# A list scheduler inside a two-layer attention kernel: charging changes of the array's tiling, new durations and new offsets

## The chip, the core and the metric

The kernel runs on one core of a Trainium2 chip. Engines: TensorE (PE) multiplies, VectorE (DVE), ScalarE (ACT) and GpSimd (POOL) do the element-wise work, SyncE (SP) issues transfers. The metric is the device time of one execution in microseconds; a run's figure is compared by its median over several runs.

## What is computed

The reference is causal attention of 8 batches, 8 heads, 576 positions, head size 64, with sparse masks, followed by a second attention per "expert" whose results are gated:

```python
scores = scale * q @ k.T                       # per batch and head
masks: heads 0-3: 0 <= i-j < 32; heads 4-7: i >= j and i % 32 == j % 32
x = softmax(masked scores) @ v                 # heads joined: x is (8, 576, 512)
logits = x @ w_gate; topk = the 2 largest of 4; w = softmax over those two
for e in range(4):
    q, k, v = x @ wq[e], x @ wk[e], x @ wv[e]  # 512 -> 64
    ye = causal_softmax(scale * q @ k.T) @ v @ wo[e]
    out += (w of e, or 0) * ye
```

All values are float32. The kernel splits activations and weights of the second layer into a high and a low part (fp32r) and multiplies high by high, low by high and high by low, so each projection step is three matmuls.

## The kernel before

Nothing in the kernel is a loop in the order of execution. Functions declare operations with `op(kind, eng, key, fn, r, w, mode, npk)` (L188): the kind's name, the engines that may do it with a duration in us for each, a key, the function that emits the instructions, the buffers read and written, the tiling of the array for PE, and for a transfer its size. `schedule()` (L219) then keeps a model clock for each engine, and step by step takes the operation that can start first; among those of one engine that are ready within 0.02 us of each other it takes the lowest key. The function of the operation is called at that moment, so each engine's queue holds its instructions in the order of the plan. On the chip semaphores keep the order of data.

The key is a due time (batch number times T = 52 plus a place within the batch) plus two offsets from the table `PRI` (L107 to L185): one for the kind, one for the kind in that batch (the key is put together in L192). `LAT` (L217) is added behind an operation's end before a reader may start. Copies out of PSUM that either ACT or DVE may do have two durations, from `act(n)` and `dve(n)` (L324, L327).

Buffers come from rings (L84): a fixed number of tiles; an operation can't start until each buffer it uses has a tile. `RB` (L308) is PSUM: eight banks of 128 x 512 floats. `PTR` (one buffer) holds transposed probabilities of the first attention, `XH` and `XL` (five each) the high and low part of that attention's result.

Operations on PE, with the lines of their matmuls and the tiling (rows x columns) that they use, for each batch:

- `stage1`, four pairs of heads, two local and two strided: `tp` transposes of q and k (L529, 64x128), `s` scores (L561, 64x64), `pt` transposes of the probabilities (L619 local, L622 strided, 64x128), `xa` probabilities times values (L656 local, 128x64; L673 strided, 64x64). Between `s` and `pt` stand mask, maximum, subtraction, exponential, sum and scaling on DVE, POOL and ACT.
- `project`: `pj`, eight of twelve matmuls (L779; L790 in the first batch, where each is cut into four parts of three), `values2`: `vp`, five of twelve (L726), all 128x128.
- `attend`, for two pairs of experts and two groups of query tiles: `s2` scores (L864, 64x128) and `s2_4` for the last tile (L844, 128x128), `t2` transposes (L918, 64x128), `acc` probabilities times values (L951, 128x64).
- `out_tile`: `yp` (L980, 128x128), its copy and its store (L989 to L992).

A transposing operation writes two PSUM banks, each emptied by a copy on ACT or DVE (L334). In a batch there are 8 `tp`, 6 `pt` and 10 `t2`. Loads (L421 weights, L475 and L482 q and k, L503 to L514 v), the small gate copy (L764) and the stores all are issued from SP's queue.

The choice among ready operations, before:

```python
for rt, o in ready:
    if rt <= first + 0.02:
        k = o.key + (MODE_PEN if e == "PE" and mode not in (None, o.mode) else 0.0)
...
if e == "PE":
    if mode not in (None, o.mode):
        d += 0.09
    elif t > free[e] + 0.05:
        d += 0.08
...
MODE_PEN = 5.0
```

Of the kernel before, what the change touches and what calls it, by code (L numbers as in the profile page):

```python
# [20 lines left out]
def attention_moe_kernel(  # L21
# [45 lines left out]
    class Buf:  # L67


        def __init__(self, ring, name, root=None):  # L70
            self.ring, self.name = ring, name
            self.root = root or self
            self.writers, self.readers, self.parts = [], [], {}
            self.t, self.nops, self.freed, self.taken = None, 0, 0.0, False

# [5 lines left out]
    class Ring:  # L81


        def __init__(self, tag, shape, dtype, bufs, pool=None, tiles=None):  # L84
            self.tag, self.bufs = tag, bufs
            if tiles is None:
                tiles = [pool.tile(shape, dtype, name=f"{tag}{i}") for i in range(bufs)]
            self.tiles, self.holder = tiles, [None] * bufs

# [18 lines left out]
        "acc": 114.0, "acc 0": -309.5, "acc 1": 334.0, "acc 2": 0.5, "acc 3": -4.0, "acc 4": 65.5,  # L108
# [13 lines left out]
        "hi_w 0": -35.5, "lo_w": 81.0, "lo_w 0": -112.0, "load_qk": 4.0, "load_qk 0": -138.0,  # L122
        "load_qk 1": -69.5, "load_qk 2": 23.0, "load_qk 3": -12.0, "load_qk 4": -31.5, "load_qk 5": 38.5,
        "load_qk 6": 39.5, "load_qk 7": 61.5, "load_v": 80.0, "load_v 0": -111.0, "load_v 1": -7.0,
        "load_v 2": -4.0, "load_v 3": 2.5, "load_v 4": 91.0, "load_v 5": 65.5, "load_v 6": 39.5,
        "load_v 7": 28.0, "load_w": -16.5, "load_w 0": 55.5, "mask": -175.5, "mask 0": 162.0, "mask 1": 75.0,
# [10 lines left out]
        "pj_lo 6": -203.5, "pj_lo 7": 167.5, "pj_out": -95.5, "pj_out 0": -139.5, "pj_out 1": 101.5,  # L137
# [186 lines left out]
    def act(n):  # L324
        return 0.15 + 0.00083 * n
# [732 lines left out]
```

## Time and profile before

| | us |
|---|---|
| median of 3 runs | 489.04 |
| lowest and highest run | 488.28, 492.18 |
| span of the profiled execution | 488.3 |
| PE busy in it | 470.8 |
| DVE, ACT, POOL busy | 338.3, 307.4, 215.3 |

The span runs from the first to the last instruction of the profiled execution. A busy PE is one on which a matmul is in flight by the profiler's model; matmuls overlap, so the rate is read from the distance between the starts of two of them. In rows of the timeline "x12" means that twelve equal instructions behind each other were merged; the first number is the start, the second how long the row lasts.

### The profile page before, as it was taken

The page shows a single profiled execution, that of the slowest core. Times are in us where ns is not written, and L with a number is a line of the kernel's source. Part 1 is how long each engine was busy: PE and PEld are TensorE (multiplying, and loading weights), DVE is VectorE, ACT ScalarE, POOL GpSimd, SP SyncE. Part 2 cuts the span into 40 slices and gives each one's busy share as a digit, 9 for nine tenths or more (in the row PEclk, how much of TensorE's full clock was granted, in tenths as well). Part 3 has the DMA queues.
Part 4 walks back from the last instruction along what each step waited for, and adds up shares of the span by engine and source line. Part 5 has one row for each costly group of instructions (what it writes and reads, how often), then busy time and mean ns, then how long its engine had stood idle before and what let it go on. Part 6 is the DMA issues. An engine that isn't in the chain of part 4 may idle for free.

```text
span 488.3 us, 17766 instructions
## 1 busy us (share of the span) xinstructions
PE 470.8 (96%) x7142; PEld 409.5 (84%) x7142; DVE 338.3 (69%) x1037; ACT 307.4 (63%) x876; POOL 215.3 (44%) x315
## 2 busy tenths in 40 slices
PE   7579899999999999999999999999999999999996
PEld 6569788889789988799987999898878998799774
DVE  5497867887778678766669557856787856635740
ACT  3487678655575487855687647737777445845742
POOL 5377643461455146641446504463086425212530
PEclk9798999999999999999999999999999999999999
DMA  7866961702166015630247403510223300100014
GB/s 145 172 170 152 203 118 54 170 1 75 46 155 135 1 48 157 164 85 2 75 119 208 130 2 83 153 49 27 76 94 84 83 1 28 65 1 1 23 66 129
DMA packets 88881, 43.36 MB, mean 89 GB/s; under 512 B 77024, under 2 KB 80480, under 8 KB 88800
## 3 DMA queue, kind: packets, MB, share of 16 engines
q1 hardware_dynamic: 88800, 42.24, 34.4%
q8 instruction: 56, 0.92, 0.8%
q14 instruction: 25, 0.20, 0.1%
HBM read 32.78 MB, written 9.44 MB: 86 GB/s over the span
## 4 chain that ended last, share of the span: by engine, by line
PE 88%; DMA 5%; SPq 4%; DVE 1%; issue 1%; ACT 0%; DVEq 0%; ACTq 0%
PE bank L779 19%; PE bank L726 12%; PE bank L980 11%; PE bank L951 10%; PE bank L864 7%; PE bank L918 7%; PE bank L561 5%; PE bank L529 4%; PE bank L656 3%; DMA nat<-in_k_dram 3%; PE bank L844 3%; PE bank L673 2%; PE bank L619 2%; SPq L421 1%; PE bank L790 1%; PE bank L622 1%
## 5 line engine op out<-in xcount | busy, mean ns | idle before, releaser
L899 POOL TENSOR_SCALAR p<-p,st,wt 128x128 f32<-128x128 f32 (+3 forms) x128 | 76.0, 608 | 88.1 <-DVE st L883 53.1
L876 ACT ACTIVATE p<-p,st 128x128 f32<-128x128 f32 (+3 forms) x128 | 71.8, 562 | 11.2 <-DVE st L871 11.1
L871 DVE CUSTOM_DVE_ANT_0 p<-bank,m_cau 128x128 f32<-128x128 f32 (+3 forms) x128 | 55.9, 485 | 13.7 <-PE bank L864 13.7
L799 ACT CAST qk<-bank 128x288 fp32r<-128x288 f32 x64 | 25.5, 400 | 47.4 <-PE bank L779 45.0
L951 PE MATMUL bank<-th,vs 128*64 128x192 f32 (+4 forms) x512 | 50.4, 339 | 0.0
L334 ACT COPY qkt<-bank 128x324 f32<-128x324 f32 (+2 forms) x110 | 40.3, 425 | 14.5 <-PE bank L529 14.0
L334 ACT COPY th<-bank 128x256 f32<-128x256 f32 (+2 forms) x102 | 40.7, 425 | 11.8 <-PE bank L918 8.3
L726 PE MATMUL bank<-wl_v,xh 128*128 128x260 f32 (+1 forms) x160 | 45.3, 283 | 1.2 <-DVE wl_v L430 1.2
L726 PE MATMUL bank<-wh_v,xh 128*128 128x260 f32 (+1 forms) x160 | 46.2, 288 | 0.0
L951 PEld LDWEIGHTS bank<-th,vs 128*64 128x64 f32 x512 | 33.9, 136 | 13.6 <-issue 6.6
L726 PE MATMUL bank<-wh_v,xl 128*128 128x260 f32 (+1 forms) x160 | 45.2, 283 | 0.0
L334 DVE COPY th<-bank 128x384 f32<-128x384 f32 (+2 forms) x58 | 28.4, 496 | 23.6 <-PE bank L918 23.1
L801 DVE TENSOR_TENSOR qkl<-bank,qk 128x288 fp32r<-128x288 f32 x64 | 28.4, 451 | 21.4 <-ACT qk L799 21.0
L918 PEld LDWEIGHTS bank<-ident,p 64*128 64x128 f32 x800 | 31.8, 138 | 11.4 <-issue 5.8
L918 PE MATMUL bank<-ident,p 64*128 64x64 f32 x800 | 41.2, 230 | 0.1
L596 POOL TENSOR_TENSOR p1l<-p1l,st 128x960 f32<-128x960 f32 (+1 forms) x18 | 29.0, 1616 | 24.5 <-DVE st L594 16.4
L587 POOL TENSOR_TENSOR p1l<-p1l,st 128x960 f32<-128x960 f32 (+1 forms) x18 | 29.0, 1614 | 23.6 <-DVE st L585 20.2
L529 PE MATMUL bank<-ident,nat 54*128 54x54 f32 (+1 forms) x636 | 30.9, 231 | 7.4 <-DMA nat<-in_k_dram 4.4
L561 PE MATMUL bank<-qkt 64*64 64x54 f32 (+1 forms) x1408 | 34.1, 242 | 2.0 <-issue 0.7
L529 PEld LDWEIGHTS bank<-ident,nat 54*128 54x128 f32 (+1 forms) x636 | 25.3, 143 | 11.8 <-issue 3.6
L779 PE MATMUL bank<-xh,wh_k 128*128 128x288 f32 x112 | 34.2, 306 | 0.0
L641 ACT CAST xh<-bank 128x320 fp32r<-128x320 f32 (+4 forms) x80 | 26.9, 376 | 11.4 <-PE bank L656 6.1
(147 smaller groups left out, 1341.3 us busy)
## 6 DMA issues: line engine op xcount, KB each, us to landing
out_dram<-ys SPq DMA_DIRECT2D x32, 256.0 KB
v<-in_v_dram SPq DMA_DIRECT2D x32, 192.0 KB
nat<-in_q_dram SPq DMA_DIRECT2D x28, 144.0 KB
nat<-in_k_dram SPq DMA_DIRECT2D x28, 144.0 KB
nat<-in_q_dram SPq DMA_DIRECT2D x32, 99.0 KB
nat<-in_k_dram SPq DMA_DIRECT2D x32, 99.0 KB
v<-in_v_dram SPq DMA_DIRECT2D x48, 54.0 KB
nat<-in_q_dram SPq DMA_DIRECT2D x16, 90.0 KB
```

The costliest lines, as they stand in the source:

```text
L334: (nc.scalar.copy if e == "ACT" else nc.vector.tensor_copy)(dst, src)
L529: nc.tensor.transpose(tp[x].t[:, w_ * (g - g0):w_ * (g - g0) + w_], blk, ident[r, r])
L561: nc.tensor.matmul(o, lhs, rhs, start=True, stop=True)
L726: nc.tensor.matmul(vp.t[:m, :NV], xx.t[:, t0:t0 + m], ww.t[:, kt, :], start=i == 0, stop=i == 11)
L779: nc.tensor.matmul(pj.t[:, :HS], ww.t[:, kt, ep * 128:(ep + 1) * 128], xx.t[:, c], start=i == 0, stop=i == 11)
L864: nc.tensor.matmul(sp[a].t[:, :nk], x.t[r, 0, q0:q0 + 128], y.t[r, 1, :nk], start=i == 0, stop=i == 2)
L871: lambda e, sp=sp, p=p, a=a, nk=nk, ci=ci: nc.vector.tensor_tensor_reduce(out=p.t[:, a, :nk], in0=sp[a].t[:, :nk], in1=m_cau[:, S - nk:], ...
L876: op("exp2", {"ACT": 0.485 + 0.00083 * nk}, k_ + 1, lambda e, p=p, a=a, ci=ci, nk=nk: nc.scalar.activation(p.t[:, a, :nk], p.t[:, a, :nk], ...
L899: lambda e, p=p, a=a, ci=ci, t=t, nk=nk: nc.gpsimd.tensor_scalar(p.t[:, a, :nk], p.t[:, a, :nk], st.t[:, 14 + ci + a:15 + ci + a], wt.t[:, ...
L918: nc.tensor.transpose(tp[hf].t[:, 64 * c:64 * c + 64], src, ident[r, r])
L951: nc.tensor.matmul(acc.t[o, c0:c0 + cn], vw, th[a].t[:, s0:s0 + cn], start=j == 0, stop=j == idx[-1], skip_group_check=True)
L980: nc.tensor.matmul(yp.t[:, :DM], xx.t[:, c0:c0 + 128], ww.t[:, ep, :], start=i == 0, stop=i == 5)
```

## The change

The set of operations, their instructions and their transfers are the same. What differs is the scheduler's model and its choice:

- Among PE's ready operations, one of another tiling counts as ready `SWITCH` later, and the window of choice on PE is `WAIT_PE`. `MODE_PEN` is 614.376 instead of 5. A change of tiling costs 0.095 us plus a lead that depends on the new tiling, instead of 0.09.
- Durations of nearly all operations and `LAT` have new values.
- Transfers are modelled in us on two lanes, of which the strided loads use one.
- `PTR`, `XH` and `XL` are handed out in the order in which their buffers were made.
- All offsets of `PRI` are new; the old ones lie between -838 and 405, the new ones reach beyond -3000 and 2800.

The diff, cut (of the offsets and of the durations only examples are shown):

```diff
+            if ring and ring.fifo:
+                ring.order.append(self)
...
+            self.fifo, self.order = False, []
...
+            if self.fifo:
+                self.order.remove(buf)
...
-        "acc": 114.0, "acc 0": -309.5, "acc 1": 334.0, "acc 2": 0.5, "acc 3": -4.0, "acc 4": 65.5,
+        "acc": 0.0, "acc 0": -1082.0, "acc 1": 1878.0, "acc 2": -874.0, "acc 3": 176.0, "acc 4": 1208.0,
...
-    LAT = {"PE": 0.22, "ACT": 0.1, "DVE": 0.1, "POOL": 0.12, "SP": 0.0}
+    LAT = {"PE": 0.2, "ACT": 0.14, "DVE": 0.12, "POOL": 0.11, "SP": 0.0}
...
-        dma_free = 0.0
+        dma = [0.0, 0.0]
...
                         if not u.taken:
+                            if u.ring.fifo and u.ring.order[0] is not u:
+                                rt = None
+                                break
                             need[u.ring] = need.get(u.ring, 0) + 1
...
-                    first = rt if first is None else min(first, rt)
-                    ready.append((rt, o))
+                    other = e == "PE" and mode not in (None, o.mode)
+                    ef = rt + (SWITCH if other else 0.0)
+                    first = ef if first is None else min(first, ef)
+                    ready.append((ef, rt, o, other))
...
-                for rt, o in ready:
-                    if rt <= first + 0.02:
-                        k = o.key + (MODE_PEN if e == "PE" and mode not in (None, o.mode) else 0.0)
+                for ef, rt, o, other in ready:
+                    if ef <= first + (WAIT_PE if e == "PE" else 0.02):
+                        k = o.key + (MODE_PEN if other else 0.0)
...
             if e == "PE":
+                lead = LEAD.get(o.mode, 0.045)
                 if mode not in (None, o.mode):
-                    d += 0.09
+                    d += 0.095 + lead
                 elif t > free[e] + 0.05:
-                    d += 0.08
+                    d += lead
...
-                dma_free = max(dma_free, t) + o.npk * 0.0014
-                o.end = max(t + d + 1.7, dma_free + 1.7)
+                for i in range(2 if o.npk > 0 else 1):
+                    dma[i] = max(dma[i], t + d) + abs(o.npk)
+                o.end = max(dma[:2 if o.npk > 0 else 1]) + 1.8
...
-    MODE_PEN = 5.0
+    MODE_PEN = 614.376
+    SWITCH, WAIT_PE = 0.104, 0.074
+    LEAD = {"128x128": 0.11, "64x128r": 0.06}
...
     def act(n):
-        return 0.15 + 0.00083 * n
+        return 0.06 + 0.00082 * n
     def dve(n):
-        return 0.14 + 0.00104 * n
+        return 0.07 + 0.00104 * n
...
-            op("lo_w", {"DVE": dve(n), "POOL": 0.06 + 0.0019 * n}, 15.5 + k_ * 0.1, lambda e, kt=kt, raw=raw: (
+            op("lo_w", {"DVE": 0.1 + dve(n), "POOL": 0.1 + 0.0025 * n}, 15.5 + k_ * 0.1, lambda e, kt=kt, raw=raw: (
...
+    for r_ in (PTR, XH, XL):
+        r_.fifo = True
...
-        op("s", {"PE": 1.0 if local else 0.75}, k0 - 11, scores, r=[qkt], w=[*sp, p[0], p[1]], mode=MQ)
+        op("s", {"PE": 0.846 if local else 0.71}, k0 - 11, scores, r=[qkt], w=[*sp, p[0], p[1]], mode=MQ)
...
-                op("exp2", {"ACT": 0.485 + 0.00083 * nk}, k_ + 1, lambda e, p=p, a=a, ci=ci, nk=nk: nc.scalar.activation(
+                op("exp2", {"ACT": 0.285 + 0.00084 * nk}, k_ + 1, lambda e, p=p, a=a, ci=ci, nk=nk: nc.scalar.activation(
```

## Rows read from the trace of the kernel before

**Rows 1.** The page: span and busy time of the engines.
```profile
span 488.3 us, 17766 instructions
...
PE 470.8 (96%) x7142; PEld 409.5 (84%) x7142; DVE 338.3 (69%) x1037; ACT 307.4 (63%) x876; POOL 215.3 (44%) x315
```

**Rows 2.** The chain that ended last: shares by engine, then one piece (start, us).
```profile
PE 88%; DMA 5%; SPq 4%; DVE 1%; issue 1%; ACT 0%; DVEq 0%; ACTq 0%
...
151.34 7.39 PE bank L726 x60
```

**Rows 3.** Busy time by stage: stage, length, each engine, granted clock, DMA share, GB/s.
```profile
0.00:60.00 60.00, 48.24 (x895) 42.12 (x897) 44.31 (x112) 35.63 (x95) 37.09 (x54) 0.91 0.77 168
60.00:450.00 390.00, 388.90 (x5950) 341.84 (x5947) 278.85 (x874) 252.33 (x730) 166.18 (x239) 1.00 0.30 79
450.00:488.30 38.30, 33.68 (x303) 25.57 (x301) 15.13 (x52) 19.47 (x53) 11.99 (x22) 0.99 0.22 70
```

**Rows 4.** TensorE's waits over the whole span: us in total, times, longest.
```profile
PE bank L529 <- DMA nat<-in_k_dram: 4.4, 3, 2.3
PE bank L529 <- DMA nat<-in_q_dram: 2.2, 2, 1.8
PE bank L1000 <- DVE p1l L342: 1.2, 1, 1.2
```

**Rows 5.** Timeline of TensorE: first and last change of tiling, short stays.
```profile
6.81 0.77 PE L529 MATMUL bank<-ident,p 64*128 64x64 f32 x18
...
40.24 0.59 PE L622 MATMUL bank<-ident,p1s 64*128 64x64 f32 x12
...
45.48 0.48 PE L619 MATMUL bank<-ident,p1l 64*96 64x64 f32 x10
...
474.31 0.53 PE L918 MATMUL bank<-ident,p 64*128 64x64 f32 x10
...
479.30 0.50 PE L980 MATMUL bank<-wh_o,oh 128*128 128x512 f32 x1
```

**Rows 6.** Timeline of TensorE: a lone transposition in a projection; twenty transposes.
```profile
67.03 0.30 PE L790 MATMUL bank<-xl,wh_k 128*128 128x288 f32 x1
67.17 0.29 PE L790 MATMUL bank<-xh,wl_k 128*128 128x288 f32 x1
67.39 0.49 PE L619 MATMUL bank<-ident,p1l 64*96 64x64 f32 x10
67.81 0.40 PE L790 MATMUL bank<-xh,wh_k 128*128 128x288 f32 x1
68.05 0.30 PE L790 MATMUL bank<-xl,wh_k 128*128 128x288 f32 x1
...
113.27 0.72 PE L619 MATMUL bank<-ident,p1l 64*96 64x64 f32 x20
113.92 0.33 PE L726 MATMUL bank<-wh_v,xh 128*64 128x260 f32 x1
```

**Rows 7.** Two exponentials in ACT's timeline; groups of copies on ACT and DVE.
```profile
108.56 0.49 ACT L876 ACTIVATE p<-p,st 128x256 f32<-128x256 f32 x1
...
109.06 0.49 ACT L876 ACTIVATE p<-p,st 128x256 f32<-128x256 f32 x1
...
L334 ACT COPY qkt<-bank 128x324 f32<-128x324 f32 x53 | 20.2, 442 | 5.6 <-PE bank L529 5.6
...
L334 DVE COPY qkt<-bank 128x324 f32<-128x324 f32 x11 | 5.2, 481 | 4.4 <-PE bank L529 4.4
```

**Rows 8.** Timelines at the end of the start: last weights' issue, first value projection.
```profile
48.55 0.91 SPq L419 DMA_DIRECT2D ys<-in_moe_wo_dram  x2
...
52.21 0.28 PE L726 MATMUL bank<-wh_v,xh 128*128 128x260 f32 x1
```

**Rows 9.** TensorE's waits from 60 to 450 us, the longer of two rows.
```profile
PE bank L561 <- issue: 0.7, 1, 0.7
```

**Rows 10.** Waits in SP's own queue: a store that waits for a copy.
```profile
SPq L992 <- ACT th L334: 33.8, 6, 20.9
```

More of the change, by code (lines that the diff above doesn't have):

```diff
@@ L233, in schedule @@
         n = 0
-        busy = {e: 0.0 for e in LAT}
         while n < len(OPS):
@@ L424, in load @@
                         dma.dma_start(dst[:, E * D:n], w_gate[r, :])
-            op("load_w", {"SP": 0.55 + 0.4 * (name == "v")}, k_, load, w=[st], npk=512)
-            op("hi_w", {"ACT": act(n)}, 15 + k_ * 0.1, lambda e, kt=kt, raw=raw: nc.scalar.copy(hi.t[:, kt, :], raw()),
+            op("load_w", {"SP": 0.45 + 0.5 * (name == "v")}, k_, load, w=[st], npk=0.6)
+            op("hi_w", {"ACT": 0.1 + act(n)}, 15 + k_ * 0.1, lambda e, kt=kt, raw=raw: nc.scalar.copy(hi.t[:, kt, :], raw()),
                r=[st], w=[hi[kt]])
-            op("lo_w", {"DVE": dve(n), "POOL": 0.06 + 0.0019 * n}, 15.5 + k_ * 0.1, lambda e, kt=kt, raw=raw: (
+            op("lo_w", {"DVE": 0.1 + dve(n), "POOL": 0.1 + 0.0025 * n}, 15.5 + k_ * 0.1, lambda e, kt=kt, raw=raw: (
                 nc.vector if e == "DVE" else nc.gpsimd).tensor_sub(lo.t[:, kt, :], raw(), f(hi.t[:, kt, :])),
@@ L485, in stage1 @@
             for src, p0 in ((q, 0), (k, 64)):
-                op("load_qk", {"SP": 0.66 if local else 1.3}, (k0 - 30 if b else hp), lambda e, src=src, p0=p0, h=h: load_qk(e, src, p0, h),
-                   w=[nat], npk=576 if local else 1000)
+                op("load_qk", {"SP": 0.67 if local else 1.25}, (k0 - 30 if b else hp), lambda e, src=src, p0=p0, h=h: load_qk(e, src, p0, h),
+                   w=[nat], npk=0.72 if local else -1.77)
         def vv():
@@ L537, in stage1 @@
         for h in range(2 if local else 1):
-            op("load_v", {"SP": 1.0 if local else 2.6}, (k0 - 25 if b else 4.0 + hp), lambda e, h=h: load_v(e, h), w=[vt], npk=864 if local else 1000)
+            op("load_v", {"SP": 1.0 if local else 2.4}, (k0 - 25 if b else 4.0 + hp), lambda e, h=h: load_v(e, h), w=[vt], npk=1.03 if local else -1.75)
         sp = [RB.new(f"s{h}_{n}") for h in range(2)]
@@ L601, in stage1 @@
                 ph, sh = [p[h] for h in range(*h_)], [st[h] for h in range(*h_)]
-                eng = {"DVE": 0.4 if step == 4 else dve(n_)}
+                eng = {"DVE": 0.34 if step == 4 else dve(n_)}
                 if step in (1, 5):
-                    eng = {"POOL": 0.06 + 0.00181 * n_}
+                    eng = {"POOL": 0.145 + 0.0017 * n_}
                 elif step == 2:
-                    eng = {"ACT": act(n_)}
+                    eng = {"ACT": 0.05 + act(n_)}
                 r_, w_ = ((ph, sh), (ph + sh, ph), (ph, ph), (ph, sh), (sh, sh), (ph + sh, ph))[step]
@@ L624, in tps2 @@
                                                 ident[r, r])
-            op("pt", {"PE": 0.06 * ni + 0.03}, k0 - 2 + 0.5 * u, tps2, r=[p[u]] if local else [p[0], p[1]], w=[*pt, ptt], mode=MR)
+            op("pt", {"PE": 0.0555 * ni if local else 0.063 * ni}, k0 - 2 + 0.5 * u, tps2, r=[p[u]] if local else [p[0], p[1]], w=[*pt, ptt], mode=MR)
             for hf in range(2):
@@ L640, in split @@
             for u, (s_, x_, n_) in enumerate(parts, u):
-                op("xh", {"ACT": act(n_)}, key, lambda e, s_=s_, x_=x_: nc.scalar.copy(x_(xh.t), s_(xa.t)),
+                op("xh", {"ACT": act(n_) + 0.04 * (not local)}, key, lambda e, s_=s_, x_=x_: nc.scalar.copy(x_(xh.t), s_(xa.t)),
                    r=[xa], w=[xh[u]])
@@ L674, in values1 @@
                                              pv2()[r, h ^ b_, b_, m, :n_], start=True, stop=True)
-            op("xa", {"PE": 0.74}, k0, values1, r=[vt, ptt], w=[*xa, *(x[u] for x in (xh, xl) for u in range(3))], mode=MQ)
+            op("xa", {"PE": 0.697}, k0, values1, r=[vt, ptt], w=[*xa, *(x[u] for x in (xh, xl) for u in range(3))], mode=MQ)
             def runs(g0, gn, rn):
@@ L757, in gate2 @@
             nc.vector.tensor_mul(w_, w_, mx.t.unsqueeze(2).to_broadcast([128, NT, E]))
-        op("gate1", {"DVE": 2.6}, key + 5 * step + 0, gate1, r=[vs[t] for t in range(NT)], w=[gt, eq, sel, mx, wt])
-        op("gate2", {"ACT": 0.25}, key + 5 * step + 0.2, lambda e: nc.scalar.activation(wt.t[:, :NT], wt.t[:, :NT], AF.Exp),
+        op("gate1", {"DVE": 1.64}, key + 5 * step + 0, gate1, r=[vs[t] for t in range(NT)], w=[gt, eq, sel, mx, wt])
+        op("gate2", {"ACT": 0.12}, key + 5 * step + 0.2, lambda e: nc.scalar.activation(wt.t[:, :NT], wt.t[:, :NT], AF.Exp),
            r=[wt], w=[wt])
-        op("gate3", {"DVE": 1.8}, key + 5 * step + 0.4, gate2, r=[wt, sel, mx], w=[wt, mx])
-        op("gate4", {"SP": 0.1}, key + 5 * step + 0.6, lambda e: nc.sync.dma_start(wt.t[64:128, NT, 0:2], wt.t[0:64, NT - 1, 1::2]),
-           r=[wt], w=[wt[1]], npk=64)
+        op("gate3", {"DVE": 0.95}, key + 5 * step + 0.4, gate2, r=[wt, sel, mx], w=[wt, mx])
+        op("gate4", {"SP": 0.6}, key + 5 * step + 0.6, lambda e: nc.sync.dma_start(wt.t[64:128, NT, 0:2], wt.t[0:64, NT - 1, 1::2]),
+           r=[wt], w=[wt[1]], npk=0.1)
         op("gate5", {"POOL": 0.2}, key + 5 * step + 0.6, lambda e: nc.gpsimd.tensor_copy(wt.t[0:64, NT, 0:2], wt.t[0:64, NT - 1, 0::2]),
@@ L791, in part @@
                                              start=kt + i == 0, stop=kt == KT - 1 and i == 2)
-                    prev = [op("pj", {"PE": 3 * 0.134}, key + step * u + 0.1 * kt, part,
+                    prev = [op("pj", {"PE": 3 * 0.132}, key + step * u + 0.1 * kt, part,
                                r=[X[b, kt][i][x] for i in range(2) for x in range(2)] + [W[nm][i][kt] for i in range(2)],
@@ L809, in diag @@
                         nc.gpsimd.tensor_copy(qk.d.t[r, i, r], f(x.t[r, 0, S - 64:]))
-            op("qd", {"POOL": 1.2}, key + step + 1, diag, r=[qk[0, 1], qk.lo[0, 1]], w=[qk.d])
+            op("qd", {"POOL": 1.08}, key + step + 1, diag, r=[qk[0, 1], qk.lo[0, 1]], w=[qk.d])
     BLK = [[(0, 0), (0, 1), (0, 2), (1, 1), (1, 2), (2, 2)], [(0, 3), (1, 3), (2, 3), (3, 3)]]
@@ L844, in mml @@
                             nc.tensor.matmul(sp.t[:, :HS], qk.d.t[:, l], r.t[:, 1, c0:c0 + HS], start=i == 0, stop=i == 2)
[L846 removed]
+                    op("s2_4", {"PE": 0.391}, k_ + 0.2 * hh, mml, r=[qk.d, qk[1, hh], qk.lo[1, hh]],
                        w=[sp, p[0]], mode=M128)
[L848 removed]
+                    op("max2_4", {"DVE": 0.1 + 0.00104 * HS}, k_ + 0.5 + 0.2 * hh,
                        lambda e, sp=sp, p=p, c0=c0, hh=hh, ci=ci: nc.vector.tensor_tensor_reduce(
@@ L853, in attend @@
                        r=[sp] + ([st["h"]] if hh else []), w=[p[0], st[t, 0] if hh else st["h"]])
-                op("exp2_4", {"ACT": 0.485 + 0.00083 * nk}, k_ + 1, lambda e, p=p, ci=ci: nc.scalar.activation(
+                op("exp2_4", {"ACT": 0.285 + 0.00084 * nk}, k_ + 1, lambda e, p=p, ci=ci: nc.scalar.activation(
                     p.t[:, :S], p.t[:, :S], AF.Exp, bias=st.t[:, ci:ci + 1], scale=-1.0,
@@ L869, in attend @@
             for a in range(2):
-                op("max2", {"DVE": 0.23 + 0.00102 * nk}, k_ + 0.5,
+                op("max2", {"DVE": 0.08 + 0.00104 * nk}, k_ + 0.5,
                    lambda e, sp=sp, p=p, a=a, nk=nk, ci=ci: nc.vector.tensor_tensor_reduce(
@@ L885, in attend @@
         kk = key + 3.6 * (len(idx) - 1) + 1.5
-        op("recip2", {"DVE": 0.4}, kk, recip, r=[st["s"]], w=[st["r"]])
+        op("recip2", {"DVE": 0.3}, kk, recip, r=[st["s"]], w=[st["r"]])
         for t in idx:
@@ L892, in attend @@
             if t == NT - 1:
-                op("scale2_4", {"POOL": 0.33 + 0.00086 * nk}, kk + 0.2, lambda e, p=p, ci=ci: nc.gpsimd.tensor_scalar(
+                op("scale2_4", {"POOL": 0.317 + 0.00085 * nk}, kk + 0.2, lambda e, p=p, ci=ci: nc.gpsimd.tensor_scalar(
                     p.t[:, :S], p.t[:, :S], st.t[:, 14 + ci:15 + ci], wt.t[:, NT, ep:ep + 1], ALU.mult, ALU.mult),
@@ L897, in attend @@
             for a in range(2):
-                op("scale2", {"POOL": 0.33 + 0.00086 * nk}, kk + 0.3 * (t - idx[0]) + 0.1 * a,
+                op("scale2", {"POOL": 0.317 + 0.00085 * nk}, kk + 0.3 * (t - idx[0]) + 0.1 * a,
                    lambda e, p=p, a=a, ci=ci, t=t, nk=nk: nc.gpsimd.tensor_scalar(
@@ L955, in attend @@
         dsts = [O[b, ep]] + ([OF[b // 2, ep]] if un else [])
-        op("acc", {"PE": cols * 4 / 2400 + 0.1}, kk + 4.5, av, r=[vs[j] for j in range(idx[-1] + 1)] + th,
+        op("acc", {"PE": cols * 4 / 2400 + 0.026}, kk + 4.5, av, r=[vs[j] for j in range(idx[-1] + 1)] + th,
            w=[acc] + [y[un if i == 0 else b % 2] for i, pair in enumerate(dsts) for y in pair], mode=MC)
@@ L981, in mm @@
                     i += 1
-        op("yp", {"PE": 6 * 0.234}, key, mm, r=need + wbufs("o"), w=[yp, ys], mode=M128)
+        op("yp", {"PE": 6 * 0.229}, key, mm, r=need + wbufs("o"), w=[yp, ys], mode=M128)
         op("yp_out", either(DM), key + 0.5, lambda e: copy(e, ys.t, yp.t[:, :DM]), r=[yp], w=[ys])
@@ L992, in store @@
                 nc.sync.dma_start(out[b, t0:t0 + 128, :], ys.t)
-        op("store", {"SP": 0.5}, key + 1, store, r=[ys], npk=128)
+        op("store", {"SP": 0.5}, key + 1, store, r=[ys], npk=0.9)
     wb = RB.new("warm")
```

34 lines of the change are left out of this document (16 added, 18 removed), and 143 rows, old and new, of the table PRI.

## The prediction

> **What bounds the kernel now.** I read the page's busy times, then busy time by stage, TensorE's waits and the chain, and only then the order of its matmuls. PE is busy for 470.8 of 488.3 us, the next engine (DVE) for 338.3, and the chain that ended last is 88% PE [rows 1, 2]. By stage [rows 3], PE is idle for 60.0 - 48.24 = 11.8 us in the first 60 us, for 390.0 - 388.90 = 1.1 us in the next 390, and for 38.3 - 33.68 = 4.6 us in the last 38, which is the eviction and store behind the last matmul. In the start, 4.4 + 2.2 = 6.6 of the 11.8 us are waits for two loads and 1.2 us the wait before the first matmul [rows 4]; 11.8 - 6.6 - 1.2 = 4.0 us are anything else.
>
> A reader who stops there says that only the start can be improved. But a full PE row doesn't say that the array computes all the time. The matmuls carry their tiling in their shapes. I count as one stay all neighbouring matmuls of one tiling (by line: 529, 619, 622, 864, 918 are 64x128; 656, 951 128x64; 561, 673 64x64; the rest 128x128). There are 287 stays, so 286 changes, from the one at 6.81 us to that at 479.30 us [rows 5]: 26 of them begin in the first 60 us, 239 from 60 to 450 and 21 behind that.
>
> What a change costs is read where a projection is interrupted by one lone transposition [rows 6]. Inside the projection a matmul starts every 0.13 to 0.14 us. From 67.17 (the last one before) to 68.05 (the second one after) 0.88 us pass. The work in it is two projection matmuls, 0.27, and ten transposing ones. Those ten cost 0.65 - 0.42 = 0.23 us, because twenty of them take 113.92 - 113.27 = 0.65 up to the next matmul of another tiling and ten take 67.81 - 67.39 = 0.42. So 0.88 - 0.27 - 0.23 = 0.38 us go for two changes, 0.19 each; the gaps that show by themselves are 0.22 for 0.13 going out (0.09) and 0.24 for 0.13 after coming back (0.11). At 0.19, 286 changes are 54 us of PE's "busy" time. That is what can be had beside the start.
>
> **The change part by part.** No instruction of computation and no transfer is added or removed; only the order in each queue, and which engine takes a copy or a weight's low part, can differ. PE's own matmuls stay what they are.
>
> 1. Weight of a change. In the old scheduler an operation of another tiling was handicapped by 5 against offsets whose standard deviation over the table is 169: three per cent of the spread, practically nothing. In the new one it is 614 against a spread of 1067, over half of it; besides, an operation of another tiling counts as ready 0.104 us later, and PE chooses within a window of 0.074 us. The time lost is charged with 0.095 + 0.045 us (0.11 in place of 0.045 for 128x128), 0.14 to 0.205, where the old one charged 0.09; the 0.19 of the rows lies within the new charge. So stays should become longer. How many go? 34 stays are shorter than 0.75 us and lie between two stays of one and the same tiling, the first at 45.48 us and the last at 474.31 us [rows 5]; such a visit merged into a neighbouring stay of its kind takes away two changes, so all 34 give 68. Not each can be moved, but 67 stays are shorter than 0.75 us in all, from 40.24 to 474.31 us [rows 5], and the other 33 can give one change each; I take 68, from 286 to about 218. Bounds: none (the handicap is outweighed by the offsets) and 68 + 33 = 101. At 0.17 us a change (between 0.10, the mean of the two gaps that show alone, and 0.19, nearer to the latter because that is the whole visit) this is -11.6 us, with bounds 0 and -19.2 (101 x 0.19).
>
> 2. Measured durations. The old table charged an exponential of 256 columns 0.485 + 0.00083 x 256 = 0.70 us on ACT, the new one 0.285 + 0.00084 x 256 = 0.50; in the trace the next one starts 109.06 - 108.56 = 0.50 us later [rows 7]. A recorded duration (0.49, and a read behind it) overlaps its neighbour, so the spacing of starts is the right charge, and the new table has it. What does that give by itself? Wrong durations give orders in which an engine waits, and PE's idle time from 60 to 450 us is 1.1 us altogether [rows 3]. So at most -1.1 there; I take 0 and count it as a reason that what is planned is what runs.
>
> 3. Loads and the start. The model of transfers now has two lanes. The first matmul of the value projection starts at 52.21 us, soon behind the issue of the last weights, 48.55 + 0.91 = 49.5 us [rows 8]; the stage moves 168 GB/s at a DMA share of 0.77 [rows 3]. Another order can't make the bytes fewer; it can fill what isn't a wait for them, 4.0 us. I take -2.5; bounds -7.3 (half of the 6.6 too) and +4.4 (as much waiting again as the longer of the two rows). PE's clock, granted 0.91 of 2.4 GHz on average here [rows 3], so 1.2 for part of the stage, goes with these waits and isn't counted again.
>
> 4. Rings in order of birth. The transposed-probability ring (one buffer) and the two rings of split activations (five each) are now taken in the order in which their buffers were declared. That adds no instruction and no wait of its own on the chip, it forbids overtaking in the plan: a pair of heads whose load is late holds all later ones. Queued behind it on PE are the transposes of its probabilities and the product with the values, and all projections of that batch wait for those. From 60 to 450 us no wait of PE for a transfer is listed, the longest being 0.7 us of issue [rows 9], so cover is there: 0, and if it were gone +4.4 as in 3.
>
> 5. The SP queue. Loads, stores and the small gate copy share it; a store waits there up to 20.9 us [rows 10], with loads queued behind it. PE doesn't notice now. If one such wait falls in front of a load that is due, the price is up to some 20 us; value 0.
>
> Sum: 488.3 - 11.6 - 2.5 = 474.2 us for the profiled execution. The runs' median, 489.04, is 0.8 above its span, so 475.0 us.
>
> **The rivals.**
>
> A, the forecast: 205 to 235 changes, a start shorter by 1 to 4 us, 475 us (469 to 481). For it: of the 67 stays under 0.75 us 57 are 64x128, a tiling that four kinds of operation (transposes of inputs, of both sorts of probabilities, and scores) could share. Against: their inputs come from DVE, ACT and POOL at different times.
>
> B, more goes: some 190 changes and 4 us of the start, 96 x 0.17 + 4 = 20.3, so 469 us or less. For it: long stays are possible, as the 60 value matmuls at 151.34 us [rows 2]. Against: such stays are of projections, which need no company.
>
> C, the plan doesn't do what it says: offsets, which differ by thousands between batches, outweigh the handicap, or a change saved in one place comes back in another; 270 to 290 changes, 489 us with the start unchanged. Against it: a handicap of 614 is not small beside 1067.
>
> D, slower: evictions become the bound. Eight PSUM banks hold four transposing operations of two banks each; one lasts 0.23 to 0.4 us on PE [rows 6], while its two copies, one on ACT and one on DVE, take 0.44 and 0.48 [rows 7], twice that where one engine has to do both. Long stays of this kind fill the banks and PE waits, where short visits between projections gave the copies time. There are 8 batches x 24 = 192 such operations; if half of them wait 0.25 us, 24 us are lost against 14.1 saved, 499 us. It decides from 14.1 / 96 = 0.15 us for each. Against it: DVE and ACT are busy for 69% and 63% only [rows 1], and no wait of PE for a copy over 0.7 us is listed in the middle [rows 9]. The Trainium skill, TensorEngine Tiling (Array Packing), section "PSUM Bottleneck", states that tiling makes TensorE faster but not the evacuation of PSUM, which may become the bottleneck.
>
> **How the numbers follow.** Chances: A 0.50, B 0.22, C 0.18, D 0.10. The likeliest is A, 475.0 us. About 1% (5 us) is what a measurement of this kernel can tell from no change. Faster by over 1%, below 484: A, B and a sixth of C, 0.75. Within 1%: the rest of C and a fifth of D, 0.17. Slower, above 494: 0.08. The range goes down through B to 463 (489.0 - 19.2 - 7.3 = 462.5) and up to 491, C with 2 us for a load that comes late; less than 2 in 10 lie outside, nearly all of it D.
>
> **What would show it.** Right: 205 to 235 changes of tiling; PE busy for 455 to 462 us instead of 470.8, with the same matmuls; PE idle still under 3 us between 60 us and the last stage; DVE and ACT busy within 10 us of 338 and 307. The value projection's first matmul before 52 us shows part 3. Wrong: 270 changes or more (C); or fewer changes, but rows of PE waiting for copies of ACT or DVE, over 10 us together (D); or PE waits for loads behind 60 us (parts 4 and 5).

## The result and the profile after

The changed kernel takes 477.82 us (median of four runs, 474.49 to 478.93) beside 489.36 us for the kernel before: ratio 0.9745, interval 0.97 to 0.9791. The forecast was 475.0. The profiled execution's span went from 488.3 to 476.9 us, by 11.4; of the four runs it is the one with the lowest mean granted clock (0.977 of 2.4 GHz), where the quickest, 474.49 us, has 0.992. Two terms of the forecast's sum were wrong in size and nearly made up for each other, and that is what the experiments are about.

The page's span and busy times after, the answer to [rows 1]:

```profile
span 476.9 us, 17806 instructions
PE 457.0 (96%) x7142; PEld 414.0 (87%) x7142; DVE 348.4 (73%) x1058; ACT 292.8 (61%) x856; POOL 214.3 (45%) x314
```

PE's busy time fell by 470.8 - 457.0 = 13.8 us with the same 7142 matmuls. DVE has 10 us more and ACT 15 us less, because DVE does 147 of the copies out of PSUM (those that either may do) instead of 127.

Busy time by stage after; it answers to [rows 3]:

```profile
core 0: us, PE busy (x) PEld busy (x) DVE busy (x) ACT busy (x) POOL busy (x), PEclk, DMA share, GB/s
0.00:60.00 60.00, 50.73 (x895) 45.42 (x896) 43.54 (x114) 33.37 (x86) 36.64 (x54) 0.89 0.81 166
60.00:450.00 390.00, 384.56 (x6033) 352.27 (x6032) 297.01 (x920) 248.81 (x743) 171.11 (x251) 0.99 0.32 80
450.00:476.90 26.90, 21.75 (x218) 16.27 (x216) 7.89 (x26) 10.60 (x28) 6.56 (x10) 0.97 0.26 88
```

Read the middle row: 6033 matmuls lie in it and the last stage needs only 26.9 us. But PE is now idle for 390.0 - 384.56 = 5.4 us there, five times the 1.1 of before. PE's waits of that stretch, the answer to [rows 9], say what ended them:

```profile
engine line waited for: us in total, times, longest us
PE bank L637 <- issue: 1.5, 1, 1.5
PE bank L936 <- issue: 1.1, 1, 1.1
PE bank L547 <- DVE th L350: 1.1, 1, 1.1
PE bank L579 <- issue: 0.6, 1, 0.6
PE bank L640 <- issue: 0.4, 1, 0.4
PE bank L969 <- issue: 0.2, 1, 0.2
PE bank L547 <- ACT pt L350: 0.2, 1, 0.2
```

Five of the seven rows say "issue": 1.5 + 1.1 + 0.6 + 0.4 + 0.2 = 3.8 us in which PE waited for nothing that the profile shows. Copies (L350) account for 1.3 us.

To size the rest I counted as in the prediction: stays of one tiling, and for each stay its length less the pure work in it (so many matmuls by the usual distance of their starts). The remainder of a stay is a change of tiling, a wait, or a slower clock.

| | before | after |
|---|---|---|
| changes of tiling | 286 | 136 |
| stays shorter than 0.75 us | 67 | 8 |
| of these between two stays of one and the same tiling | 34 | 0 |
| remainder in the first 60 us | 26.1 us | 25.2 us |
| remainder of stays begun from 60 to 450 us | 42.5 us (239 stays) | 32.8 us (103 stays) |
| of it above 0.17 us, in stays with over 0.3 | 2.3 us | 13.9 us |
| remainder behind 450 us | 8.6 us | 7.7 us |

So 150 changes went, not 68. At the prediction's 0.17 us that is 25.5 us; 13.9 - 2.3 = 11.6 us came back as waits in the middle. The start gave 0.9.

The 13.9 us lie in few places. Six us (each less 0.17 us for the change) are in the five stays with the "issue" stops; 3.1 us in three stays behind a pause of PE, part of which ran at the lower clock (shown below); 1.6 us in the stay with the 1.1 us wait for a copy; 3.1 us are spread over six others.

The longest stop, in the timeline of after:

```profile
147.09 0.99 PE L579 MATMUL bank<-qkt 64*64 64x54 f32 x48
148.02 0.37 PE L637 MATMUL bank<-ident,p1l 64*96 64x64 f32 x6
149.86 0.60 PE L637 MATMUL bank<-ident,p1l 64*96 64x64 f32 x14 [1.47 <-issue]
```

PE stops in the middle of an operation, between matmul 6 and 7 of twenty that have the same inputs and the same bank. No semaphore lies there. In the transfers of 147 to 148 us one row stands out, and the page gives its queue's total:

```profile
q8 instruction: 1, 0.02, 7.7%
...
q8 instruction: 56, 0.92, 0.8%
```

One piece of 0.92 / 56 = 0.016 MB of the program itself started at 147.18 us, and PE went on at 149.86, 2.68 us later. The other four stops end 2.65, 2.48, 2.66 and 2.65 us behind the start of such a piece. Counting weight loads and matmuls in order, the stops come behind numbers 4968, 6233, 8254, 9769 and 10021; between neighbours lie 5, 8, 6 and 1 times 252 to 253. The dense stretch ahead of this stop is scores, 48 matmuls in 0.99 us.

The clock in two stretches behind pauses of PE (granted share in the third column from the end):

```profile
140.60:143.80 3.20, 3.20 (x100) 3.10 (x95) 2.28 (x8) 0.84 (x4) 1.79 (x1) 0.50 0.67 150
151.00:154.00 3.00, 3.00 (x26) 2.88 (x25) 2.37 (x7) 2.05 (x5) 0.00 (x0) 0.50 0.81 176
```

0.50 is 1.2 GHz. The first follows the wait that ended at 138.42, the second the stop that ended at 149.86. PE counts as fully busy in both, so the busy row hides this loss.

The wait that ended at 138.42 begins on DVE. Timeline of after, POOL, DVE and PE:

```profile
136.42 1.28 POOL L614 TENSOR_TENSOR p1s<-p1s,st 128x648 f32<-128x648 f32 x1 [0.44 <-DVE st L612]
136.46 1.25 DVE L900 TENSOR_SCALAR st<-st 128x3 f32<-128x3 f32 x1
137.75 0.18 DVE L901 RECIPROCAL st<-st 128x3 f32<-128x3 f32 x1
137.84 0.53 DVE L350 COPY th<-bank 128x384 f32<-128x384 f32 x1
138.43 0.40 PE L547 MATMUL bank<-ident,nat 64*128 64x64 f32 x5 [1.06 <-DVE th L350]
```

An addition of a constant to 128 x 3 numbers, 167 ns in the median, lasts 1.25 us, exactly until POOL's operation beside it is over. The copy that PE needs stands behind it in DVE's queue. The Trainium skill, SBUF — State Buffer, section "SBUF: two separate sides", says that VectorE in some modes and GpSimd share a pair of ports which one of them holds for a whole instruction while the other is fully blocked; these rows agree, though they don't show which mode the addition runs in. Of the 32 such additions in after, the six that end 21 to 24 ns behind a POOL operation last 0.19 to 1.25 us, the other 26 take 0.15 to 0.2.

### The profile page after: what moved, and what is told of

Read it like the earlier page. It is cut to its first block, busy times and chain, and to the rows that moved or that the text cites. A ratio compares the mean times of both kernels' runs of the same rounds, so it can differ in the third digit from the quotient of the medians.

```text
span 476.9 us, 17806 instructions
## 1 busy us (share of the span) xinstructions
PE 457.0 (96%) x7142; PEld 414.0 (87%) x7142; DVE 348.4 (73%) x1058; ACT 292.8 (61%) x856; POOL 214.3 (45%) x314
## 4 chain that ended last, share of the span: by engine, by line
PE 85%; DVE 5%; issue 3%; DMA 3%; POOL 1%; SPq 1%; ACT 1%; POOLq 0%; ACTq 0%; DVEq 0%
PE bank L797 19%; PE bank L744 12%; PE bank L998 9%; PE bank L969 8%; PE bank L882 7%; PE bank L579 5%; PE bank L936 5%; PE bank L547 4%; PE bank L674 3%; PE bank L808 3%; PE bank L862 3%; PE bank L691 3%; DMA v<-in_v_dram 2%; PE bank L637 2%; PE bank L1018 1%
## 5 line engine op out<-in xcount | busy, mean ns | idle before, releaser
L917 POOL TENSOR_SCALAR p<-p,st,wt 128x256 f32<-128x256 f32 (+3 forms) x128 | 76.5, 614 | 78.6 <-DVE st L901 53.4
L969 PE MATMUL bank<-th,vs 128*64 128x192 f32 (+4 forms) x512 | 49.0, 336 | 0.2 <-issue 0.2
L350 DVE COPY th<-bank 128x384 f32<-128x384 f32 (+2 forms) x62 | 30.0, 488 | 23.9 <-PE bank L936 22.9
L350 ACT COPY th<-bank 128x256 f32<-128x256 f32 (+2 forms) x98 | 40.2, 437 | 7.1 <-PE bank L936 6.4
L936 PEld LDWEIGHTS bank<-ident,p 64*128 64x128 f32 x800 | 33.8, 139 | 9.2 <-issue 5.6
L579 PE MATMUL bank<-qkt 64*64 64x54 f32 (+1 forms) x1408 | 36.9, 249 | 3.8 <-ACT qkt L350 1.5
L350 ACT COPY qkt<-bank 128x324 f32<-128x324 f32 (+2 forms) x90 | 33.4, 434 | 8.4 <-PE bank L547 8.2
L579 PEld LDWEIGHTS bank<-qkt 64*64 64x64 f32 x1408 | 32.0, 147 | 6.2 <-ACT qkt L350 3.0
L797 PE MATMUL bank<-xh,wl_q 128*128 128x288 f32 x112 | 33.1, 295 | 0.0
L797 PE MATMUL bank<-xh,wl_k 128*128 128x288 f32 x112 | 33.0, 295 | 0.0
```

Source lines behind the costliest of these rows:

```text
L350: (nc.scalar.copy if e == "ACT" else nc.vector.tensor_copy)(dst, src)
L579: nc.tensor.matmul(o, lhs, rhs, start=True, stop=True)
L797: nc.tensor.matmul(pj.t[:, :HS], ww.t[:, kt, ep * 128:(ep + 1) * 128], xx.t[:, c], start=i == 0, stop=i == 11)
L917: lambda e, p=p, a=a, ci=ci, t=t, nk=nk: nc.gpsimd.tensor_scalar(p.t[:, a, :nk], p.t[:, a, :nk], st.t[:, 14 + ci + a:15 + ci + a], wt.t[:, ...
L936: nc.tensor.transpose(tp[hf].t[:, 64 * c:64 * c + 64], src, ident[r, r])
L969: nc.tensor.matmul(acc.t[o, c0:c0 + cn], vw, th[a].t[:, s0:s0 + cn], start=j == 0, stop=j == idx[-1], skip_group_check=True)
```

## The experiments

**Weighing and offsets apart.** The prediction let the weight of a change do the work and gave the new offsets no term. Three kernels fill the table of four: the new scheduler with the old offsets without and with weighing, and the new offsets without weighing.

```diff
     PRI = {
-        "acc": 0.0, "acc 0": -1082.0, ...
+        "acc": 114.0, "acc 0": -309.5, ...
...
-    MODE_PEN = 614.376
-    SWITCH, WAIT_PE = 0.104, 0.074
+    MODE_PEN = 0.0
+    SWITCH, WAIT_PE = 0.0, 0.02
```

Old offsets, no weighing (both parts of the diff):

> The changed kernel with the offsets of before and without weighing (no handicap, no later readiness for another tiling); its durations, transfer model and rings stay. 297 changes of tiling. Theory 1 (the forecast's term: each change saved is worth 0.17 us wherever it is saved): about 488 us, as before, which has 286 changes. Theory 2 (a saved change is given back as waits unless the offsets are found for it): it only says that this one and the next are equal; by its own plan 482 us, and with the 16 to 20 us that the chip adds to the plans of both known kernels, 498 to 502 us.

Old offsets, weighing (the first part alone):

> As the one before, but with weighing as in the changed kernel; 161 changes, 136 fewer. Theory 1: 136 x 0.17 = 23 us less than without weighing. Theory 2: within 5 us of it, with 15 us or more of new waits of TensorE in its trace.

New offsets, no weighing (the second part alone):

> The changed kernel with its own offsets and no weighing; 315 changes, 179 more than the changed kernel's 136. Theory 1: 179 x 0.17 = 30 us more than the changed kernel, 508 us. Theory 2: changes cost as much, but part of the waits (14 us in the changed kernel) goes too, so 18 to 30 us more, 496 to 508 us. If the offsets alone made the change faster it would be near 478 us.

| | no weighing | weighing |
|---|---|---|
| old offsets | 495.12 us, 297 changes | 494.49 us, 161 changes |
| new offsets | 497.76 us, 315 changes | 477.82 us, 136 changes |

The ratios to the kernel before are 1.0129 (1.0074 to 1.0184), 1.0112 (1.0065 to 1.016) and 1.0168 (1.0123 to 1.0213) for the three. Weighing alone takes 136 changes away and 0.6 us; the new offsets alone cost 2.6 us; both together gain about 17.3 us. Busy time from 60 to 450 us shows why, for old offsets without weighing, old offsets with it, and new offsets without it:

```profile
60.00:450.00 390.00, 388.10 (x5904) 341.43 (x5905) 275.57 (x872) 250.02 (x737) 168.67 (x247) 1.00 0.31 77
```

```profile
60.00:450.00 390.00, 380.83 (x5949) 343.78 (x5948) 260.24 (x832) 247.46 (x744) 164.83 (x236) 0.99 0.32 80
450.00:492.90 42.90, 33.32 (x304) 26.01 (x302) 18.66 (x70) 20.64 (x61) 12.82 (x26) 0.94 0.12 38
```

```profile
60.00:450.00 390.00, 388.10 (x5879) 337.69 (x5877) 279.57 (x890) 247.65 (x726) 169.52 (x248) 1.00 0.30 75
```

Without weighing PE is idle for 1.9 us with either table. With weighing and the old offsets it is idle for 9.2 us in the middle and 9.6 behind it, twice what the last stage had before [rows 3]. The longest of its waits, by operand:

```profile
PE bank L638 <- POOL p1s L612: 4.0, 1, 4.0
...
PE bank L934 <- POOL p L915: 4.2, 6, 1.7
```

(the first from 60 to 450 us, the second behind it). Transposes wait for probabilities that POOL scales. The same count of stays gives 21.6 us of waits from 60 to 450 us and 13.2 behind it, of which some 4.7 are the eviction and store behind the last matmul that every one of these kernels has: enough to take back what 136 changes save at 0.17 us, 23 us. So the weighing alone sheds the changes, and the offsets have to be found for it, so that operands are ready when a long stay asks for them.

**What a change costs.** The kernel before, with 88 lone transposes of one tiling put ahead of projections of the other, into a part of the bank that nobody reads:

```diff
+                if m == 128:
+                    nc.tensor.transpose(vp.t[:, 320:384], ident[0:64, :], ident[0:64, 0:64])
...
+                nc.tensor.transpose(pj.t[:, 320:384], ident[0:64, :], ident[0:64, 0:64])
```

> The kernel before with one lone transposition of 64 rows, written into unused columns of the bank, ahead of each value projection of 128 rows and each query or key projection behind the first batch: 88 more small matmuls, of which some 62 to 69 stand between two stays of 128x128, so 125 to 145 more changes, in an order that is otherwise the same. At 0.17 to 0.19 us a change and 0.03 us for each transposition: 24 to 30 us more than before. If a change costs only the 0.09 to 0.11 us of one visible gap and the rest of it is hidden: 14 to 18 us more.

It took 516.09 us, ratio 1.0546 (1.0504 to 1.0589), 27 us for 132 more changes (286 to 418; some of the transposes stand where a change was already). The control puts in as many transposes of 128 rows, which change nothing in the tiling:

```diff
-                    nc.tensor.transpose(vp.t[:, 320:384], ident[0:64, :], ident[0:64, 0:64])
+                    nc.tensor.transpose(vp.t[:, 320:448], ident, ident)
...
-                nc.tensor.transpose(pj.t[:, 320:384], ident[0:64, :], ident[0:64, 0:64])
+                nc.tensor.transpose(pj.t[:, 320:448], ident, ident)
```

> Control for the visits: the kernel before with 88 more small matmuls in the same places, but of 128 rows and 128 columns, so that the tiling doesn't change. If the visits cost because of the change of tiling: at most 88 x 0.1 = 9 us more than before, most likely 5. If they cost because a projection is interrupted by any matmul with other weights: some 25 us more, as with the visits.

498.18 us, ratio 1.0167 (1.0132 to 1.0202): 498.18 - 489.86 (the kernel before beside it) = 8.3 us, 0.09 each. The difference is 27.0 - 8.3 = 18.7 us over 132 changes, 0.14 us each, and 27.0 / 132 = 0.20 if the small transposes had cost nothing. The prediction's 0.17 lies between. In the timelines, first with a change and then without:

```profile
155.50 0.28 PE L728 MATMUL bank<-wl_v,xh 128*128 128x260 f32 x1
155.72 0.27 PE L725 MATMUL bank<-ident 64*128 64x64 f32 x1
155.92 0.39 PE L728 MATMUL bank<-wh_v,xh 128*128 128x260 f32 x1
156.14 0.29 PE L728 MATMUL bank<-wh_v,xl 128*128 128x260 f32 x1
```

```profile
155.68 0.28 PE L728 MATMUL bank<-wl_v,xh 128*128 128x260 f32 x1
155.80 0.27 PE L725 MATMUL bank<-ident 128*128 128x128 f32 x1
155.83 0.36 PE L728 MATMUL bank<-wh_v,xh 128*128 128x260 f32 x1
156.03 0.28 PE L728 MATMUL bank<-wh_v,xl 128*128 128x260 f32 x1
```

From the last projection matmul ahead of the visit to the second one behind it 0.64 us pass with a change of tiling and 0.35 without; PE counts as busy for over 99% of the middle in both.

**Is it DVE's load?** After has 10 us more on DVE, and a small addition there stood in front of a copy. The additions of 1e-9 ahead of three kinds of reciprocal can be left out, on after and, as a control, on the kernel before; another kernel keeps the additions and makes long sums shorter.

```diff
-                nc.vector.tensor_scalar_add(R[2], R[1], EPS)
-                nc.vector.reciprocal(R[2], R[2])
+                nc.vector.reciprocal(R[2], R[1])
...
-            nc.vector.tensor_scalar_add(mx.t, mx.t, EPS)
...
-            nc.vector.tensor_scalar_add(st.t[:, 14:14 + ncol], st.t[:, 8:8 + ncol], EPS)
-            nc.vector.reciprocal(st.t[:, 14:14 + ncol], st.t[:, 14:14 + ncol])
+            nc.vector.reciprocal(st.t[:, 14:14 + ncol], st.t[:, 8:8 + ncol])
```

After without the additions:

> The changed kernel in its own order, without the additions of 1e-9 to the sums of exponentials ahead of each reciprocal (each sum holds an exponential of 0, so it is at least 1 and float32 doesn't change by the addition). They occupy DVE for 5.3 + 5.2 + 4.1 + 2.9 + 1.6 = 19.1 us, some for over 1 us each. If the waits given back come from DVE being full where the plan bunches its work: 3 to 7 us less than the changed kernel. If from PSUM banks, ACT or POOL: within 2 us of it.

The kernel before without them:

> The kernel before in its own order without the same additions (17.9 us of DVE). TensorE is idle for 1.1 us from 60 to 450 us there, so whichever engine the waits of the changed kernel come from: within 2 us of before.

After with sums over a quarter of the keys:

```diff
-                nc.vector.tensor_reduce(R[1], P, axis=mybir.AxisListType.X, op=ALU.add)
+                nc.vector.tensor_reduce(R[1], P[..., :nk // 4], axis=mybir.AxisListType.X, op=ALU.add)
```

> The changed kernel in its own order, but the sums of the first attention's exponentials on DVE read only a quarter of the keys: some 22 of the 31.8 us of that line go, in 32 operations of up to 1.1 us. If DVE's queue is what TensorE waits for: 3 to 8 us less than the changed kernel; if not, within 2 us of it.

After without additions took 474.49 us, ratio 0.9677 (0.9643 to 0.9711), 3.3 us under after; the kernel before without them 487.98, ratio 0.9973 (0.9943 to 1.0003), no change that can be told; the shorter sums 476.84, ratio 0.9732 (0.9708 to 0.9756), one us under after and no difference that its interval shows. The pages' busy rows of the first and the third:

```profile
PE 451.6 (96%) x7142; PEld 409.7 (87%) x7142; DVE 330.1 (70%) x986; ACT 292.6 (62%) x856; POOL 213.2 (45%) x314
```

```profile
PE 456.1 (96%) x7142; PEld 413.1 (87%) x7142; DVE 330.9 (70%) x1058; ACT 293.3 (62%) x856; POOL 213.9 (45%) x314
```

Both have some 18 us less on DVE and get 3.3 and 1.0 us from it. The first just meets its mark of 3 to 7 us, but its interval still touches after's (0.97), and the kernel before got 2.0 us from the same edit, no change that can be told; the second stays under its mark. So DVE's load is not what mainly holds after up. By the count of stays the waits from 60 to 450 us go from 13.9 to 10.3 and 9.9. Without the additions the wait for the copy on DVE is off the list; with the shorter sums it is still there, 0.6 us of it. Both stretches at 1.2 GHz are gone from the middle in both (the granted share there is 1.00); as the clock of after differs from run to run, it isn't shown that the edits did this. But the "issue" stops stay in both, behind the very same numbers of weight loads and matmuls (4968, 6233, 8254 and 10021), and without the additions they are longer: six of at least 0.5 us from matmul to matmul, 6.1 us together, where after has five and 5.0 us. The longest without the additions:

```profile
144.61 0.37 PE L636 MATMUL bank<-ident,p1l 64*96 64x64 f32 x6
147.13 0.59 PE L636 MATMUL bank<-ident,p1l 64*96 64x64 f32 x14 [2.15 <-issue]
```

**Do the stops follow the operation or the count of instructions?** The seven warm-up matmuls of 256 columns at the start become 28 of 64; the same columns, 84 more weight loads and matmuls ahead of everything:

```diff
-        for _ in range(7):
-            nc.tensor.matmul(wb.t[:, :256], ones[:, :128], ones, start=True, stop=True)
+        for i in range(28):
+            nc.tensor.matmul(wb.t[:, 64 * (i % 4):64 * (i % 4) + 64], ones[:, :128], ones[:, 64 * (i % 4):64 * (i % 4) + 64],
+                             start=True, stop=True)
```

> The changed kernel with its seven first dummy matmuls of 256 columns cut into 28 of 64 columns: 84 more instructions in TensorE's queue ahead of everything, the same columns, the order otherwise the same. In the changed kernel TensorE stops within an operation, waiting for no semaphore, at its weight loads and matmuls number 4968, 6233, 8254, 9769 and 10021, each time about 2.65 us behind the start of a 16 KB transfer of its instructions. If it waits for instructions, the stops stay near these numbers (within 10), so they come 84 instructions earlier in the work, at other matmuls; some may vanish and others appear where it runs densely. If they belong to the operations (operands, banks), they stay at the same matmuls, at numbers higher by 84. The time within 3 us of the changed kernel's.

The stops moved to other operations and kept to the count. Behind 60 us there are four, behind numbers 4719, 6739, 8254 and 10277. 8254 is a number of after too, and stands for another operation here, as all of after's work has a number higher by 84; the others are after's 4968, 6233 and 10021 less 249, plus 506 and plus 256, one or two blocks off. The count is exact when the semaphore instructions in PE's queue are counted too: all 38 stops of at least 0.45 us behind 60 us in the twelve kept traces lie at place 193 or 194 of a block of 256, in after with 5058, 6337, 8386, 9921 and 10177 entries ahead of the matmul that goes on, here with 4801, 6849, 8386 and 10433, and in the kernel before with 3009 (its stop at 90.30 us). All four are in scores now, the densest stretches; two of them:

```profile
145.56 1.01 PE L579 MATMUL bank<-qkt 64*64 64x96 f32 x48
148.42 0.33 PE L579 MATMUL bank<-qkt 64*64 64x54 f32 x7 [1.85 <-issue]
...
204.40 1.11 PE L579 MATMUL bank<-qkt 64*64 64x54 f32 x61
207.34 0.20 PE L579 MATMUL bank<-qkt 64*64 64x54 f32 x1 [1.83 <-issue]
```

The pieces of the program ahead of them start at 145.81 and 204.53 us, 2.61 and 2.81 before PE goes on. That settles the cause: PE is stopped by the supply of its own instructions. The Trainium skill, Runtime: NRT & Kernel Launch, section "Instruction fetch mechanics", says that the queue of instructions is refilled in blocks of 256 and 16 KiB and calls the cost of a block's end mostly hidden. The size and the spacing of 256 agree with these runs; "hidden" holds outside dense stretches only.

The time was missed: 486.73 us, ratio 0.9933 (0.9908 to 0.9959), 9 us over after in place of at most 3. Part of it comes from the start. Small matmuls take long there, as the first row of PE in the two kernels shows (this one, then after):

```profile
1.25 12.21 PE L1018 MATMUL bank<-p1l 128*128 128x64 f32 x56 [1.25 <-DVE p1l L358]
```

```profile
1.25 6.32 PE L1018 MATMUL bank<-p1l 128*128 128x256 f32 x14 [1.25 <-DVE p1l L358]
```

Comparing the same matmul in both traces, the lag is 6.4 us at the fiftieth, 4.4 at the 900th, at about 60 us, and 7.2 at the 3600th, behind the stop at 205.29. So 4.4 of the 7.7 us by which its span is longer are the longer warm-up, and about 3 are put down to the longer stops (7.0 us together instead of 5.0) with a lower clock behind the first two, read in this kernel's busy time by stretch:

```profile
150.00:156.00 6.00, 6.00 (x149) 5.76 (x148) 4.41 (x10) 3.17 (x10) 1.79 (x1) 0.50 0.66 162
208.00:211.00 3.00, 3.00 (x16) 3.00 (x14) 2.54 (x8) 1.20 (x3) 0.10 (x1) 0.50 0.58 162
```

**An order that knows of the supply.** After without additions, with a table of offsets found anew under a scheduler that charges 254 weight loads and matmuls with at least 3.5 us:

```diff
+                d += STOP.get(npe, 0.0)
+                npe += 1
...
+    STOP = {306: 0.183363636, 387: 0.386666667, 435: 0.163633333}
```

(and the new table, and shorter durations for the three operations that lost an addition).

> The kernel after without the additions of 1e-9 ahead of the reciprocals (as in e6), and with a new table of offsets, found with a scheduler that also charges the instruction supply: 254 weight loads and matmuls in less than 3.5 us cost the difference. 139 changes of tiling are planned, as many as after has. If the supply is what stops TensorE in dense stretches, the stops without a semaphore behind 60 us fall from five, 5.0 us together, to at most three, 2 us together, and the time is 466 to 471 us. If the stops have another cause they stay at 4 us or more and the time is that of e6, 474 us, or above.

474.22 us, ratio 0.9699 (0.9655 to 0.9744): a miss, no better than the 474.49 of the old order without additions, and with it the fastest here. Five stops without a semaphore are left behind 60 us, 4.2 us together (6.1 in the old order without additions), two of them now inside projections and the longest behind scores again:

```profile
85.95 1.57 PE L589 MATMUL bank<-qkt 64*64 64x54 f32 x89
89.41 0.33 PE L589 MATMUL bank<-qkt 64*64 64x54 f32 x5 [1.89 <-issue]
```

89 scores in 1.57 us, then a stop where the scheduler planned none; the piece of the program ahead of it began at 86.82, 2.59 us before PE went on. By the marks of the expectation, 4 us or more of stops and the time of the old order would speak for another cause; but these five too lie at place 193 or 194 of a block of 256, so it is the plan's floor that failed. In the twelve kept traces no piece starts less than 3.38 us behind the one before, and after's ten closest pairs lie 3.6 to 4.2 us apart; a floor of 3.5 us for 254 is at the very edge of that. Whether a higher one would plan better is not tested, and what starts a piece when it starts is open.

## Why the prediction was right

The time was right by a sum whose two largest terms were wrong: that they nearly made up for each other is luck. What held is the mechanism of the first, fewer changes of tiling at the price that was read.

1. Weight of a change: the price of 0.17 us held (0.14 to 0.20 by the two kernels with more transposes). The number was mis-sized, "I take 68", with 101 as the bound; it was 150. The step that failed is the source of the number. I counted which of the old plan's short visits could be merged, as if the plan were mended; it was made anew. And I compared the handicap of 614 with the spread of the offsets, where the diff said something stronger: an operation of another tiling counts as ready 0.104 us later, and the window is 0.074. The prediction names both figures and draws nothing from them. As long as one of the same tiling can start now, no other is even compared, whatever its offset. A stay thus goes on until nothing of its kind is ready. The old offsets show it: 161 changes with weighing, 297 without. (Of the 286 changes before, 25 and not 26 begin in the first 60 us, and 22 and not 21 behind 450; no sum uses that.)

2. What comes back: the prediction put it wholly into rival D, at 0.10, and none into the forecast. 11.6 us came back, between the forecast's nothing and D's 24. D's mechanism, evictions that fill the banks, was not it: PE's rows for copies come to 1.3 us behind 60 us, against the 10 that the prediction set as its mark. The largest part, 6 us, is a mechanism that no rival had: dense stays outrun the supply of instructions. It could have been suspected from the trace of before: a stop of this kind in scores, at 90.30 us, is the 0.7 us of issue in [rows 9], which I read as cover.

3. Durations (0): no run takes them alone. New scheduler and durations with old offsets and no weighing cost 1.29%, so they bring nothing without a table made for them; what they bring with one is not shown.

4. The start: -2.5 forecast, -0.9 by the count. The value projection begins at 52.06 us, not 0.2 earlier than before [rows 8]; the rows of waits for loads and for operands changed places (PE's waits in the first 60 us, beside [rows 4]):

```profile
PE bank L691 <- DMA v<-in_v_dram: 1.6, 1, 1.6
PE bank L579 <- ACT qkt L350: 1.5, 3, 0.7
PE bank L547 <- DMA nat<-in_k_dram: 1.4, 2, 1.2
PE bank L1018 <- DVE p1l L358: 1.2, 1, 1.2
PE bank L579 <- DVE st L611: 1.0, 2, 0.8
```

In these rows and those of before, waits for loads fell from 6.6 to 3.0 us, and waits for what ACT and DVE make of them took their place.

5. Rings in order of birth (0) and SP's queue (0): no wait of PE for a transfer is listed behind 60 us, so neither cost anything. No run takes the rings' order alone, but the new scheduler with that rule taken out gives the same plan, all 2443 operations in the same order, so its share is 0 exactly.

Of the marks set in "What would show it" only PE's busy time (457.0, in 455 to 462) was met. The changes (136, not 205 to 235), PE's idle time in the middle (5.4, not under 3), the start of the value projection (52.06, not before 52), ACT (14.6 us less) and, by a tenth, DVE (10.1 more) were missed. The sum by the measured sizes is 488.3 - 25.5 + 11.6 = 474.4; the 2.5 us up to 476.9 are spread over many stays and my count gives them no cause.

## What to carry to other kernels

Read a scheduler's rule of readiness before its weights: a penalty wider than the window excludes, however small it is beside the offsets. Changes of TensorE's tiling are worth some 0.17 us each and stand in no idle row, but an order that saves them must be found together with the order of the engines that supply its operands; the weighing alone gave 0.6 us, with offsets found for it 17.3 (or 11.5 against the kernel before). And when small matmuls are packed closer, look for rows of "issue" in the middle of an operation: they come in steps of whole blocks of instructions.

## What was not expected of the hardware

- PE's instruction supply shows: stops of 0.5 to 2.4 us inside operations, ending 2.2 to 3.5 us behind the start of a 16 KB piece of the program, always at one place of a block of 256 entries of its queue, most of them in or behind stretches where a matmul starts every 15 to 21 ns.
- A pause of PE can cost more than its length: behind four of 1.3 to 2.1 us from matmul to matmul, in after and in the kernel with the longer warm-up, it ran 3 to 7 us at 1.2 GHz, while its busy row showed 100%. It isn't the length alone: behind 2.4 us in the kernel without additions, and 1.3 at 306.57 us in after, the clock stayed at 2.4 GHz.
- A DVE operation on three numbers per partition took 1.25 us in place of 0.17 and ended 23 ns behind a POOL operation on 648; six of 32 ended so, 21 to 24 ns behind.
- A warm-up of 28 matmuls of 64 columns took 12.2 us where seven of 256 columns, the same columns in all, took 6.3.
